# Local attention values: both halves of the sequence in one 64-row product on block-diagonal weights that ScalarE spreads, and weights converted in place

## The chip, the core and the metric

The kernel runs on one NeuronCore of a Trainium2 chip. Its engines are TensorE (PE; its weight loads stand as PEld), VectorE (DVE), ScalarE (ACT), GpSimd (POOL) and SyncE (SP, which issues most of the transfers). The metric is the device time of one execution in microseconds (us); below, it is 401.14 us, the median of three runs (398.07 to 405.84).

## The reference

For 8 batches and 8 heads of 576 positions and 64 numbers each, two attentions are added: a coarse one on means of four positions, and a local one in which a position sees the three before it and the three behind it. The sum goes through a gated causal convolution block.

```python
out_d = sm_attn(q_d, k_d, v_d)            # means over factor = 4 positions, 144 x 144
out_up = np.repeat(out_d, factor, axis=2)
mask = np.abs(pos[:, None] - pos[None, :]) < factor
scores = np.where(mask, scale * q @ k.T, -1e9)
out_local = softmax(scores) @ v
x = (out_up + out_local)                   # -> (8, 576, 512)
gate = sigmoid(causal depthwise convolution of x, 5 taps)
result = (gate * (x @ w_val)) @ w_out
```

w_val, w_out and the taps come in double precision.

## The kernel before

The attention runs in 16 steps. A step i has two pairs of heads (p = 2i and 2i + 1), so four heads. The projections (x @ w_val and h @ w_out) run in blocks of 504 positions, each in pieces of three products per 128 rows: high part by high part, by low part, and low by high (lines 1024 to 1026, tiles `val` and `out`).

**One step.** `sla` and `slb` (lines 682 and 693) make the local scores: the sequence is cut into 24 blocks of 24 queries, each against 30 keys; the tile `sl` holds four combinations of pair and half of the sequence in its four groups of 32 partitions, 12 blocks each for two heads. DVE takes the maximum (`mx`), subtracts it (`sub`, into the tile `ex`), ACT makes the exponentials, DVE sums, inverts, scales (`norm`) and transposes in 32 x 32 squares (`turn`, line 743, tile `pt`). `sd` (line 769) makes the coarse scores, with maximum, exponentials (line 789, into one of two tiles `pd`), scaling (`cnorm`, line 813 on ACT or 815 on DVE) and transpose (`cturn`, line 819, tile `pdt`). `odp` (line 885) makes the coarse values in the tiles `x`, one for each pair, and ACT copies them out (`oc`, line 898, tile `od`). `xa` and `xb` (line 845) then make the local values into the same tiles: for each of 12 blocks, four groups of 32 partitions and two heads, a product with 30 rows, 64 columns of weights from `vw` and 24 moving columns from `pt`; `xa` takes six of the 12 blocks, `xb` the others. DVE adds coarse and local values (`xt`, line 857, 128 x 576 for each pair) when `xb` is done. From there on come a split into high and low part (`xh`, line 916; `xl`, line 920), five convolution taps (lines 929 and 935) and the gate (line 946).

**The weights.** Eight chunks `raw` (in a ring of four buffers, tag `hhl`) come as 64-bit numbers. ACT takes fields of each out (`fld`, lines 971 to 973) into two other tiles, DVE puts them together (`val`, line 976), ACT and DVE or POOL make high and low part (lines 1002 and 1005).

**What sets the order.** `tensor_order()` lists TensorE's work: in `TURN` the scores of step i + 1 stand ahead of the values of step i, with pieces of projection between. A planner then simulates all engines with costs and due times (the numbers in the calls of `op`), lets TensorE take a later entry of the list when one has to wait, picks DVE, POOL or ACT where an operation can go to either, and writes every engine's instructions in a fixed order. It also counts instructions: `CODE` of them make a block of code, for which it assumes a time `FETCH`, and it puts off a phase of many short instructions when it would run out of code by more than `BEAR`. `free` names what must be done before a buffer is used again.

## Time and profile before

| | us |
|---|---|
| median of three runs | 401.14 (398.07 to 405.84) |
| the profiled execution, its time | 400.16 |
| its span, first to last instruction | 398.4 |
| PE busy | 356.5 |
| DVE busy | 309.2 |
| ACT busy | 198.6 |
| POOL busy | 89.7 |

The span is the time between the first and the last instruction of that one execution; the rest of its time lies around it. Busy time is an average over an opening (loads, weight conversion, first steps), a long steady part, and an end in which only projections are left. A PE that is busy can be at half its clock, so the granted clock (1.00 is 2.4 GHz, 0.50 is 1.2 GHz) is read beside it.

### The profile page before, as it was taken

The page shows a single profiled execution, that of the slowest core. Times are in us where ns is not written, and L with a number is a line of the kernel's source. Part 1 is how long each engine was busy: PE and PEld are TensorE (multiplying, and loading weights), DVE is VectorE, ACT ScalarE, POOL GpSimd, SP SyncE. Part 2 cuts the span into 40 slices and gives each one's busy share as a digit, 9 for nine tenths or more (in the row PEclk, how much of TensorE's full clock was granted, in tenths as well). Part 3 has the DMA queues.
Part 4 walks back from the last instruction along what each step waited for, and adds up shares of the span by engine and source line. Part 5 has one row for each costly group of instructions (what it writes and reads, how often), then busy time and mean ns, then how long its engine had stood idle before and what let it go on. Part 6 is the DMA issues. An engine that isn't in the chain of part 4 may idle for free.

```text
span 398.4 us, 15755 instructions
## 1 busy us (share of the span) xinstructions
PE 356.5 (89%) x7055; PEld 279.4 (70%) x7055; DVE 309.2 (78%) x481; ACT 198.6 (50%) x508; POOL 89.7 (23%) x97
## 2 busy tenths in 40 slices
PE   5585659869997989999989999979999999999996
PEld 3464536647775668778667777757777877878996
DVE  7897759993897959998967979995988894935720
ACT  1297259563653544556555544473556462524321
POOL 3223326343123410232103042502240030000000
PEclk9886888987999989999998999998999999999999
DMA  8999997988697979988988979998841301102012
GB/s 226 299 334 233 343 274 154 229 179 203 177 249 174 212 190 218 252 201 209 246 194 181 232 198 268 200 229 197 197 116 55 135 0 52 55 3 77 29 46 74
DMA packets 23476, 71.14 MB, mean 179 GB/s; under 512 B 3185, under 2 KB 9585, under 8 KB 23409
## 3 DMA queue, kind: packets, MB, share of 16 engines
q1 hardware_dynamic: 17504, 52.39, 45.7%
q0 software_dynamic: 5616, 17.50, 24.4%
q8 instruction: 55, 0.90, 1.0%
q10 hardware_dynamic: 288, 0.26, 0.2%
q14 instruction: 13, 0.10, 0.1%
HBM read 60.69 MB, written 9.44 MB: 176 GB/s over the span
## 4 chain that ended last, share of the span: by engine, by line
PE 73%; DVE 11%; issue 7%; DMA 4%; ACT 3%; SPq 1%; ACTq 0%; DVEq 0%
PE out L1024 10%; PE x L845 9%; PE val L1024 8%; PE out L1026 8%; PE out L1025 8%; PE val L1025 7%; PE val L1026 7%; PE sl L693 5%; PE x L885 4%; DMA qk<-in_qk 4%; PE sd L769 4%; DVE gp L935 3%; PE sl L682 1%; DVE h L1052 1%; ACT pd L789 1%
## 5 line engine op out<-in xcount | busy, mean ns | idle before, releaser
L935 DVE SCALAR_TENSOR_TENSOR gp<-xt,cw,gp 128x576 f32<-128x576 f32 x128 | 101.8, 826 | 0.4
L1024 PE MATMUL val<-xhs,wh_v 128*128 128x504 f32 (+1 forms) x160 | 64.5, 403 | 1.5 <-ACT xhs L916 1.5
L1025 PE MATMUL val<-xhs,wl_v 128*128 128x504 f32 (+1 forms) x160 | 60.1, 376 | 2.7 <-issue 2.7
L1024 PE MATMUL out<-hhl,wh_o 128*128 128x504 f32 (+1 forms) x144 | 60.4, 419 | 0.1
L1026 PE MATMUL val<-xls,wh_v 128*128 128x504 f32 (+1 forms) x160 | 60.4, 377 | 0.0
L1026 PE MATMUL out<-hhl,wh_o 128*128 128x504 f32 (+1 forms) x144 | 56.5, 393 | 0.0
L1025 PE MATMUL out<-hhl,wl_o 128*128 128x504 f32 (+1 forms) x144 | 56.3, 391 | 0.0
L845 PEld LDWEIGHTS x<-pt,vw 30*64 30x64 f32 x3072 | 35.3, 133 | 23.9 <-issue 22.1
L857 DVE TENSOR_TENSOR xt<-x,od 128x576 f32<-128x576 f32 x32 | 23.1, 745 | 36.7 <-PE x L845 36.7
L845 PE MATMUL x<-pt,vw 30*64 30x24 f32 x3072 | 39.2, 220 | 12.4 <-issue 12.2
L1115 ACT ACTIVATE ob<-out 128x504 f32<-128x504 f32 (+2 forms) x40 | 21.9, 550 | 42.2 <-PE out L1026 33.9
L693 PE MATMUL sl<-qk 128*24 128x60 f32 x1536 | 30.9, 232 | 12.2 <-DMA qk<-in_qk 7.8
L1066 ACT CAST hhl<-h 128x504 fp32r<-128x504 f32 (+2 forms) x44 | 22.0, 518 | 35.4 <-DVE h L1052 31.4
L693 PEld LDWEIGHTS sl<-qk 128*24 128x24 f32 x1536 | 28.4, 113 | 14.7 <-issue 11.1
L1024 PEld LDWEIGHTS val<-xhs,wh_v 128*128 128x128 f32 x160 | 30.5, 191 | 9.9 <-issue 2.7
L1026 PEld LDWEIGHTS val<-xls,wh_v 128*128 128x128 f32 x160 | 30.5, 191 | 9.1 <-issue 3.2
L576 POOL DMA_DIRECT2D vs<-in_vgr x21 | 18.6, 887 | 79.1 <-DMA vs<-in_vgr 79.1
L1072 POOL TENSOR_TENSOR hhl<-h,hhl 128x504 fp32r<-128x504 f32 (+1 forms) x16 | 20.8, 1306 | 68.8 <-ACT hhl L1066 68.8
L1052 DVE SCALAR_TENSOR_TENSOR h<-gp,val 128x288 f32<-128x288 f32 (+6 forms) x64 | 26.6, 448 | 11.1 <-PE val L1026 10.9
L916 ACT CAST xhs<-xt 128x576 fp32r<-128x576 f32 (+4 forms) x40 | 21.9, 573 | 26.4 <-DVE xt L857 26.2
L1024 PEld LDWEIGHTS out<-hhl,wh_o 128*128 128x128 f32 x144 | 28.3, 196 | 8.0 <-issue 2.3
L1025 PEld LDWEIGHTS val<-xhs,wl_v 128*128 128x128 f32 x160 | 30.7, 192 | 3.8
(82 smaller groups left out, 603.3 us busy)
## 6 DMA issues: line engine op xcount, KB each, us to landing
qk<-in_qk SPq DMA_DIRECT2D x64, 291.0 KB, 8.6
vw<-in_vw SPq DMA_DIRECT2D x16, 768.0 KB, 6.3
qs<-in_qkr POOLq DMA_DIRECT2D x18, 576.0 KB, 9.4
out_t<-ob SPq DMA_DIRECT2D x32, 252.0 KB, 4.8
vs<-in_vgr POOLq DMA_DIRECT2D x21, 320.0 KB, 7.8
qs<-in_qkr SPq DMA_DIRECT2D x6, 576.0 KB, 11.5
vs<-in_vgr SPq DMA_DIRECT2D x7, 320.0 KB, 7.1
raw_v<-in_w_val SPq DMA_DIRECT2D x4, 512.0 KB, 6.9
```

Of the source, the lines that this page charges most:

```text
L693: nc.tensor.matmul(out=sc[32 * q : 32 * q + BQ, 2 * KW * g : 2 * KW * (g + 1)].rearrange("p (h k) -> p h k", h=2), lhsT=t[:, 1, 3 + blk : ...
L845: nc.tensor.matmul(out=s["x", q % 2][64 * hd : 64 * hd + 64, q // 2, BQ * g : BQ * g + BQ], lhsT=s["vw"][32 * q : 32 * q + KW, 2 * g + hd] ...
L857: nc.vector.tensor_tensor(out=xt[:, 4:].rearrange("p (e j r) -> p e j r", e=2, r=FAC), in0=s["x", pr][:, :, 0:HALF].rearrange("p e (j r) - ...
L916: nc.scalar.copy(out=xhs[:, c, g : g + t - f], in_=s["xt"][:, 4 + f : 4 + t])
L935: nc.vector.scalar_tensor_tensor(out=s["gp"], in0=s["xt"][:, k : k + S], scalar=cw[:, c, k : k + 1], in1=s["gp"], op0=ALU.mult, op1=ALU.add,)
L1024: nc.tensor.matmul(out=o, lhsT=wh[:, d, col], rhs=his[d], start=d == 0, stop=False)
L1025: nc.tensor.matmul(out=o, lhsT=wl[:, d, col], rhs=his[d], start=False, stop=False)
L1026: nc.tensor.matmul(out=o, lhsT=wh[:, d, col], rhs=los[d], start=False, stop=d == NC - 1)
L1052: nc.vector.scalar_tensor_tensor(out=t["h"][:, cs], in0=st[b * NC + c]["gp"][:, f:e], scalar=1.0, in1=box["o"][:, cs], op0=ALU.add, op1=AL ...
L1066: nc.scalar.copy(out=t["hh"][:, cuts[n]], in_=t["h"][:, cuts[n]])
L1072: eng.tensor_tensor(out=t["hl"][:, cs], in0=t["h"][:, cs], in1=t["hh"][:, cs].bitcast(F32), op=ALU.subtract)
L1115: nc.scalar.mul(t["ob"][:, cs], box["o"][:, cs], 0.5)
```

## The change

The local values are made by products of 64 rows instead of 30. The pair of heads now decides which 64 partitions a score lies in, and the half of the sequence which 32 of these. After the transpose ACT copies `pt` into a new tile `pt2`, which has two groups of 24 columns: the first half's rows go to the first group and the second half's rows to the second, and the rest, zeroed once, stays zero. So one product with 64 rows and 48 moving columns gives both halves of the sequence. `xa` and `xb` have half as many products, of twice the columns. The four copies (`spr0` to `spr3`, 32 partitions each) wait for `turn` and for `xa` and `xb` of the step before; `xa` waits for them.

The result of `xa` and of `xb` lies in a bank of its own, and the addition becomes four operations of 128 x 288 (`xu` after `xa`, `xt` after `xb`) in place of two of 128 x 576. The two tiles `pd` become one, so that the exponentials of the coarse scores wait for `cturn` of the step before. The weight fields are written into the 64-bit chunk itself, which is held until the low part is made. Five costs of the planner and its rule for a switch between kinds of work differ; they have an effect through the order alone.

```diff
-CODE, FETCH, BEAR = 256, 4500, 300
+CODE, FETCH, BEAR = 256, 5500, 300
-        return 0 if a == b else 95
+        return 0 if a == b else (95 if b != "P" else 30)
-    pds = [cpool.tile([P, NG, 32 * NB], F32, name=f"pd{i}") for i in range(2)]
+    pt2 = cpool.tile([P, 2 * NI, 2, BQ], F32, name="pt2")
+    pd = cpool.tile([P, NG, 32 * NB], F32, name="pd")
+        nc.gpsimd.memset(pt2, 0.0)
...
-                        t = st[pair[q % 2]]["qk"]
-                        blk = HALF * (q // 2) + BQ * (NI // 2 * part + g)
+                        t = st[pair[q // 2]]["qk"]
+                        blk = HALF * (q % 2) + BQ * (NI // 2 * part + g)
...
+        def spread(q):
+            def run():
+                r = slice(32 * q, 32 * q + 32)
+                nc.scalar.copy(out=pt2[r, :, q % 2], in_=s["pt"][r, :, 0:BQ])
...
-        op(("turn", i), "DVE", 870, turn, [("norm", i)], free=[("xa", i - 1), ("xb", i - 1)])
+        op(("turn", i), "DVE", 870, turn, [("norm", i)], free=spreads(i - 1))
+        for k, q in zip(spreads(i), range(4)):
+            op(k, "ACT", 560, spread(q), [("turn", i)], free=[("xa", i - 1), ("xb", i - 1)])
...
-            op(k, "ACT", 283, exp(g), [("cbi", i)] + exps[:g][:1], free=[("cturn", i - 2)])
+            op(k, "ACT", 283, exp(g), [("cbi", i)] + exps[:g][:1], free=[("cturn", i - 1)])
...
-                for g in range(NI // 2 * part, NI // 2 * (part + 1)):
-                    for q in range(4):
-                        for hd in range(2):
+                for g in range(NI // 2):
+                    n = 2 * (NI // 2 * part + g)
+                    for pr in range(2):
+                        for hd, r in enumerate((LO, HI)):
                             nc.tensor.matmul(
-                                out=s["x", q % 2][64 * hd : 64 * hd + 64, q // 2, BQ * g : BQ * g + BQ],
-                                lhsT=s["vw"][32 * q : 32 * q + KW, 2 * g + hd],
-                                rhs=s["pt"][32 * q : 32 * q + KW, 2 * g + hd, 0:BQ],
+                                out=s["x", pr][r, part, 0:HALF].rearrange("p (e g j) -> p e g j", e=2, j=BQ)[:, :, g],
+                                lhsT=s["vw"][(LO, HI)[pr], n + hd],
+                                rhs=pt2[(LO, HI)[pr], n + hd],
...
-        op(("raw", q), "SP", 620, dma, free=[("fld", q - RAWB)], size=P * 512 * 8)
-        op(("fld", q), "ACT", 1700, fields, [("raw", q)], free=[("wlo", q - 2), ("val", q - 1)])
+        op(("raw", q), "SP", 620, dma, free=[("wlo", q - RAWB)], size=P * 512 * 8)
+        op(("fld", q), "ACT", 1700, fields, [("raw", q)])
```

TensorE in step 5, from the last coarse products through two pieces of projection into `xa`, before (a row that ends in x2 stands for the two heads; `out1_0` is a tile of block 1's result):

```order
L885 MATMUL x1_5_2082<-pdt5_1982,vs2_841 64x145 x2
L1024 MATMUL out1_0_1976<-hhl1_3_1984,wh_o_95 128x504
L1025 MATMUL out1_0_1976<-hhl1_3_1984,wl_o_96 128x504
L1026 MATMUL out1_0_1976<-hhl1_3_1984,wh_o_95 128x504
L1024 MATMUL out1_1_1987<-hhl1_3_1984,wh_o_95 128x504
L1025 MATMUL out1_1_1987<-hhl1_3_1984,wl_o_96 128x504
L1026 MATMUL out1_1_1987<-hhl1_3_1984,wh_o_95 128x504
L845 MATMUL x0_5_2081<-pt5_1937,vw5_1605 64x24 x2
L845 MATMUL x1_5_2082<-pt5_1937,vw5_1605 64x24 x2
```

The same place of the changed kernel:

```order
L902 MATMUL x1_5_1857<-pdt5_1778,vs2_702 64x145 x2
L1040 MATMUL out1_0_1782<-hhl1_3_1780,wh_o_93 128x504
L1041 MATMUL out1_0_1782<-hhl1_3_1780,wl_o_94 128x504
L1042 MATMUL out1_0_1782<-hhl1_3_1780,wh_o_93 128x504
L1040 MATMUL out1_1_1792<-hhl1_3_1780,wh_o_93 128x504
L1041 MATMUL out1_1_1792<-hhl1_3_1780,wl_o_94 128x504
L1042 MATMUL out1_1_1792<-hhl1_3_1780,wh_o_93 128x504
L858 MATMUL x0_5_1856<-pt2_76,vw5_1408 64x2x24 x2
L858 MATMUL x1_5_1857<-pt2_76,vw5_1408 64x2x24 x2
```

The two pieces stay where they were. The rows of line 845 go on to 24 for `xa`, those of line 858 to 12, and each of the latter has two groups of 24 columns.

ACT between the exponentials of step 11's and of step 12's local scores, before (`ex` is the tile of the local weights, `od` the copy of the coarse values, `hhl` and `xhs` high parts, `gp` the gate):

```order
L725 ACTIVATE ex_75<-ex_75 128x24x30
L783 ACTIVATE cbi11_3742<-cmx11_3730 128x5
L789 ACTIVATE pd1_77,csm11_3744<-sd11_3701,cbi11_3742 128x144 x5
L1066 CAST hhl4_0_3774<-h4_0_3736 128x504
L898 COPY od0_10_3780<-x0_10_3748 128x144
L898 COPY od1_10_3782<-x1_10_3749 128x144
L946 ACTIVATE gp18_3673<-gp18_3673 128x576
L1066 CAST hhl4_1_3848<-h4_1_3841 128x504
L946 ACTIVATE gp19_3690<-gp19_3690 128x576
L1066 CAST hhl4_2_3928<-h4_2_3875 128x504
L916 CAST xhs_86<-xt0_82 128x144
```

The changed kernel from the same `hhl` of block 4 on:

```order
L1082 CAST hhl4_2_3447<-h4_2_3418 128x504
L933 CAST xhs_86<-xt0_82 128x144
L933 CAST xhs_86<-xt0_82 128x432
L946 ACTIVATE gp20_3467<-xt0_82,cw_90 128x576
L754 COPY pt2_76<-pt11_3460 32x24x24 x3
L825 ACTIVATE pd_77<-pd_77,crs11_3542 128x144 x5
L1082 CAST hhl4_3_3563<-h4_3_3534 128x252 x2
L754 COPY pt2_76<-pt11_3460 32x24x24
L933 CAST xhs_86<-xt1_83 128x144
```

The four copies of line 754 stand among the casts, with five scalings of `pd` and two casts between the third and the fourth. Over the whole program the planner also deals some work out anew: of the 40 subtractions `xl`, DVE has 32 instead of 22 and POOL 8 instead of 18; of the subtractions `hlo`, DVE has 9 fewer and POOL 9 more; three of the 16 `norm` go from DVE to POOL; and of the 16 `cnorm`, ACT has 14 instead of 11 (five instructions each).

## Rows read from the trace of the kernel before

**Rows 1.** The page's busy times: engine, us, share of the span, instructions.

```profile
PE 356.5 (89%) x7055; PEld 279.4 (70%) x7055; DVE 309.2 (78%) x481; ACT 198.6 (50%) x508; POOL 89.7 (23%) x97
```

**Rows 2.** Busy us of each engine by stretch of the span, granted clock, transfers' share, GB/s.

```profile
36.00:90.00 54.00, 39.16 (x938) 28.36 (x937) 46.23 (x67) 32.19 (x76) 22.86 (x21) 0.85 0.94 236
90.00:343.00 253.00, 242.87 (x5034) 188.15 (x5033) 208.95 (x330) 130.49 (x348) 57.64 (x57) 0.97 0.75 181
```

**Rows 3.** Waits of PE from 90 to 343 us: line, released by, us, times, longest.

```profile
PE x L845 <- issue: 5.3, 3, 2.4
PE val L1025 <- issue: 2.7, 2, 2.3
PE sd L769 <- issue: 1.2, 3, 0.7
PE sl L693 <- issue: 0.4, 1, 0.4
```

**Rows 4.** The longest waits of PE on issue from 0 to 90 us.

```profile
PE x L845 <- issue: 6.9, 2, 3.5
PE sl L693 <- issue: 3.9, 1, 3.9
PE out L549 <- issue: 3.8, 1, 3.8
```

**Rows 5.** The longest wait of DVE from 90 to 343 us.

```profile
DVE xt L857 <- PE x L845: 25.6, 9, 5.2
```

**Rows 6.** PE in order of time: start us, us, line, operation, count [idle before].

```profile
119.60 1.15 PE L845 MATMUL x<-pt,vw 30*64 30x24 f32 x96
120.69 0.50 PE L1024 MATMUL val<-xhs,wh_v 128*128 128x504 f32 x1
...
129.65 0.80 PE L693 MATMUL sl<-qk 128*24 128x60 f32 x48
130.38 0.50 PE L1024 MATMUL out<-hhl,wh_o 128*128 128x504 f32 x1
...
157.71 1.43 PE L769 MATMUL sd<-qs 64*32 64x144 f32 x40
159.06 0.50 PE L1024 MATMUL val<-xhs,wh_v 128*128 128x504 f32 x1
...
209.48 0.47 PE L845 MATMUL x<-pt,vw 30*64 30x24 f32 x18 [1.54 <-issue]
```

**Rows 7.** The page's queue of code transfers: packets, MB, share of 16 engines.

```profile
q8 instruction: 55, 0.90, 1.0%
```

**Rows 8.** Two of three stretches at half clock behind such waits, columns as above.

```profile
144.80:148.20 3.40, 3.40 (x10) 2.69 (x9) 0.83 (x2) 0.68 (x1) 0.63 (x2) 0.50 0.51 190
...
267.70:271.10 3.40, 3.40 (x9) 2.64 (x8) 0.65 (x1) 0.45 (x1) 0.86 (x1) 0.50 0.64 184
```

**Rows 9.** Groups of instructions by line: count, busy us, mean ns, idle before.

```profile
L845 PE MATMUL x<-pt,vw 30*64 30x24 f32 x3072 | 39.2, 220 | 12.4 <-issue 12.2
L857 DVE TENSOR_TENSOR xt<-x,od 128x576 f32<-128x576 f32 x32 | 23.1, 745 | 36.7 <-PE x L845 36.7
L813 ACT ACTIVATE pd<-pd,crs 128x144 f32<-128x144 f32 x55 | 18.0, 404 | 9.9 <-DVE crs L807 9.7
L971 ACT ACTIVATE bits_v<-raw_v 128x512 uint16<-128x512 uint32 x4 | 3.2, 790 | 0.0
L973 ACT ACTIVATE a_v<-raw_v 128x512 f32<-128x512 f32 x4 | 2.6, 660 | 0.0
```

**Rows 10.** Groups by line with shapes kept apart: DVE from PSUM at 288 columns, ACT.

```profile
L1052 DVE SCALAR_TENSOR_TENSOR h<-gp,val 128x288 f32<-128x288 f32 x16 | 7.2, 450 | 1.4 <-PE val L1026 1.4
L916 ACT CAST xhs<-xt 128x576 fp32r<-128x576 f32 x24 | 15.9, 668 | 17.8 <-DVE xt L857 17.7
```

**Rows 11.** DVE and then PE in step 7, in order of time.

```profile
171.92 0.97 DVE L743 STREAM_TRANSPOSE pt<-ex 128x768 f32<-128x768 f32 x1
...
182.33 1.15 PE L845 MATMUL x<-pt,vw 30*64 30x24 f32 x96
```

More of the change, by code (lines that the diff above doesn't have):

```diff
@@ L669, in tile_two_scale_attn_gated_conv, with spreads @@
     at = {}
+    def spreads(i):
+        return [(f"spr{q}", i) for q in range(4)]
     def local_scores(i):
@@ L789, in run @@
                 nc.scalar.activation(
-                    out=pds[i % 2][:, g, 0:SD],
+                    out=pd[:, g, 0:SD],
                     in_=s["cs"][:, g],
@@ L863, in combine @@
             return run
-        op(("xa", i), "PE", 850, mm(0), [("vw", i), ("turn", i), ("odp", i), ("oc0", i), ("oc1", i)], cols=(576, 290), code=192)
-        op(("xb", i), "PE", 850, mm(1), [("xa", i)], cols=(576, 290), code=192)
+        op(("xa", i), "PE", 700, mm(0), [("vw", i), ("odp", i), ("oc0", i), ("oc1", i)] + spreads(i), cols=(1150, 290), code=96)
+        op(("xb", i), "PE", 700, mm(1), [("xa", i)], cols=(1150, 290), code=96)
         for pr in range(2):
             p = 2 * i + pr
-            op(
-                (f"xt{pr}", i), "DVE", 680, combine(pr), [("xb", i), (f"oc{pr}", i)],
-                free=[("tap3", p - 4), ("xl", p - 4)],
-            )
+            for part, (k, x) in enumerate((("xu", "xa"), ("xt", "xb"))):
+                op(
+                    (f"{k}{pr}", i), "DVE", 390, combine(pr, part), [(x, i), (f"oc{pr}", i)] + [(f"xu{pr}", i)] * part,
+                    free=[("tap3", p - 4), ("xl", p - 4)],
+                )
     def coarse_av(i):
@@ L903, in coarse_av @@
         op(
-            ("odp", i), "PE", 1200, mm, [("vb", i) if i < 2 else ("vs3", i // 2), ("cturn", i)],
-            banks=[("a", [(f"xt{pr}", i)]) for pr in range(2)], cols=(1450, 144), code=80,
+            ("odp", i), "PE", 1250, mm, [("vb", i) if i < 2 else ("vs3", i // 2), ("cturn", i)],
+            banks=[("a", [(f"xu{pr}", i), (f"xt{pr}", i)]) for pr in range(2)], cols=(1450, 144), code=80,
         )
@@ L963, in tile_two_scale_attn_gated_conv, with f64_parts @@
     whl = {}
-    def f64_parts(src, bits, at):
+    def f64_parts(src):
         w = src.bitcast(U32).rearrange("p (n two) -> p n two", two=2)
-        lo, hi = w[:, :, 0], w[:, :, 1].bitcast(F32)
-        low, top = (bits.bitcast(t).rearrange("p (n two) -> p n two", two=2)[:, :, i] for i, t in enumerate((U16, I16)))
+        lo, at = w[:, :, 0], w[:, :, 1]
+        hi = at.bitcast(F32)
+        low, top = (src.bitcast(t).rearrange("p (n four) -> p n four", four=4)[:, :, i] for i, t in enumerate((U16, I16)))
         def fields():
@@ L992, in fields @@
         def fields():
-            t["a"] = work.tile([P, 512], U32, tag="h", name=f"a_{nm}{d}")
-            bits = work.tile([P, 512], U32, tag="ob", name=f"bits_{nm}{d}")
-            t["f"] = f64_parts(t["raw"], bits, t["a"])
+            t["f"] = f64_parts(t["raw"])
             t["f"][0]()
@@ L1082, in val_unit @@
         two = units.index((j, c)) - 2
-        held = [("wlo", 2 * NC - 2), ("wlo", 2 * NC - 1)] if j == 0 else []
         op((f"h{c}", j), "DVE", 75 + w * 574 // 504 + 60 * (len(batches) - 1), gated,
            [(f"v{c}.{pieces(j) - 1}", j)] + [("gate", b * NC + c) for b in batches],
-           free=held + [(f"hlo{units[two][1]}.{n}", units[two][0]) for n in range(2) if two >= 0])
+           free=[(f"hlo{units[two][1]}.{n}", units[two][0]) for n in range(2) if two >= 0])
         hfree = [(f"o{NC - 1}.{NC - 1}", j - 1) if j <= NFULL else (f"v{NC - 1}.{NC - 1}", NFULL - 1)]
         if j == 0:
-            hfree = [("fld", 2 * NC - 1 - i) for i in range(RAWB)]
+            hfree = [("wlo", 2 * NC - 1 - i) for i in range(RAWB)]
         if c == NC - 1 and j < NFULL:
@@ L1143, in cw_in @@
         nc.sync.dma_start(out=cw_raw, in_=conv_w)
-    cw_low, cw_at = (cpool.tile([P, NC * 5], U32, name=n) for n in ("cw_low", "cw_at"))
-    cw_parts = f64_parts(cw_raw, cw_low, cw_at)
+    cw_parts = f64_parts(cw_raw)
     def cw_value():
         cw_parts[1]()
-        nc.vector.tensor_copy(out=cw2, in_=cw_at.bitcast(F32))
+        nc.vector.tensor_copy(out=cw2, in_=cw_parts[2])
     op(("cwf", 0), "SP", 620, cw_in, size=P * NC * 5 * 8)
@@ L1210 @@
     v2 = v.reshape(NSTEP, 2, 2, S, D)
-    vp = np.pad(v2, ((0, 0), (0, 0), (0, 0), (3, 5), (0, 0)))
-    vw = np.stack([vp[:, :, :, BQ * g : BQ * g + 32] for g in range(2 * NI)], axis=3)
-    vw = vw.reshape(NSTEP, 2, 2, 2, NI, 32, D).transpose(0, 3, 1, 5, 4, 2, 6).reshape(NSTEP, P, 2 * NI, D)
+    vp = np.pad(v2, ((0, 0), (0, 0), (0, 0), (3, 3), (0, 0)))
+    vw = np.stack([vp[:, :, :, BQ * g : BQ * g + KW] for g in range(2 * NI)], axis=3)
+    vw = np.pad(vw, ((0, 0), (0, 0), (0, 0), (0, 0), (0, 32 - KW), (0, 0)))
+    vw = vw.reshape(NSTEP, 2, 2, 2, NI, 32, D).transpose(0, 1, 3, 5, 4, 2, 6).reshape(NSTEP, P, 2 * NI, D)
     vg = np.pad(v.reshape(B, 2, 2, 2, SD, FAC, D), ((0, 0), (0, 0), (0, 0), (0, 0), (0, 32 * NB - SD), (0, 0), (0, 0)))
```

47 lines of the change are left out of this document (25 added, 22 removed).

## The prediction

> **What bounds the kernel now.** I read the busy times by stretch first. From 90 to 343 us PE is busy for 242.9 of 253 us, DVE for 209.0 (83%), ACT for 130.5 (52%) [rows 2]. So in the long steady part TensorE sets the pace, and DVE comes next. From 36 to 90 us it is the other way round: DVE 46.2 of 54 us, PE 39.2, and PE's clock is 0.85 of full speed on the mean [rows 2].
>
> Then the waits. From 90 to 343 us PE waits for no other engine; all four rows name "issue", where the profile sees nothing that was waited for, 9.6 us in sum [rows 3]. DVE's longest wait there is for PE, in `xt`, 25.6 us [rows 5]. Before 90 us the three long waits on issue are 6.9, 3.9 and 3.8 us [rows 4].
>
> What is it that PE waits for on "issue"? One queue of transfers carries instructions, 55 packets of 0.90 MB, so 16.4 KB each [rows 7]. PE and PEld have 14,110 instructions [rows 1], 256.5 for each packet. So I read these packets as TensorE's code, 256 instructions at a time. A wait on issue cuts an x phase in two: 18 of its 96 products come 1.54 us late [rows 6]. Such a phase of 192 instructions takes 1.09 us, and a piece of projection has six instructions in a good half microsecond. Dense phases use code up fastest, and `xa` and `xb` are the densest. The Trainium skill's page "Runtime: NRT & Kernel Launch", Instruction fetch mechanics, agrees on blocks of 256 instructions, but says that the fetch is hidden behind the sequencer's own pace. By that the waits have another cause, and the change leaves them; the second rival below is that case.
>
> Three stretches of 3.4 us from 90 us on have a granted clock of 0.50, so 1.2 GHz instead of 2.4, and they come up to 4 us after a wait in an x phase [rows 8].
>
> **The change, part by part.**
>
> *x phases.* Before, 96 products go in 1.09 us, from 119.60 to the next projection at 120.69 [rows 6]. What limits them? Two phases with four places of the array in use show what columns cost: 40 products of 144 columns take 1.35 us, 48 of 60 columns 0.73 us [rows 6]. That is ten rounds of four at 144 and twelve at 60; the difference, 0.62 us for 720 columns, gives 0.86 ns a column and leaves 0.11 us for the ends of a phase. An x phase of before has eight places and twelve rounds of 24 columns, 0.25 us by columns, so columns don't limit it. It goes at (1.09 - 0.11) / 96 = 10.2 ns a product, which I take as the pace of issue. Afterwards there are 48 products of 48 columns in four places: twelve rounds, 12 x 48 x 0.86 = 0.50 us by columns and 48 x 10.2 = 0.49 us by issue, with the ends 0.60 us. That is the lower bound. The upper bound takes the 82 ns of a round of before as the latency of one place, to which 24 more columns add 21 ns: 12 x 103 ns and the ends, 1.34 us. I take 0.70: near the lower end, since the phase of 144 columns runs in the same pattern of four places without such a latency, and a little over it, since two limits that lie together seldom overlap fully. So 0.39 us less for each of 32 phases. 26 of them (13 steps) lie behind 90 us: **10.1 us**. The other six give 2.3, of which I count a quarter, as in the opening below: **0.6**.
>
> The Trainium skill's page "TensorEngine Tiling (Array Packing)", Theoretical Speedup, speaks against this: its gain goes with the number of tiles, and the change has four where there were eight, half filled with zeros. If a phase went by places, it would take twice its 0.98 us; the trace has a quarter of that as column time, so here it doesn't.
>
> *Waits on issue.* PE's instructions fall by 3,072 to 11,038, or 43 packets; an x phase has 96 instead of 192. Of the 9.6 us behind 90 us, 5.3 are in x phases and 2.7 in a projection [rows 3], which I take to be behind one. I take three quarters of these 8.0 as gone and a third of the other 1.6: **6.6 us** (bounds 0 and 9.6).
>
> *Clock.* Each stretch of 3.4 us at half clock costs 1.7 us. If two of three waits before them go, so do they: **3.4 us** (bounds 0 and 5.1).
>
> *The opening.* 14.6 us of waits on issue lie before 90 us [rows 4], but DVE is busy for 86% of the stretch from 36 on, so I count a quarter: **3.7 us** (bounds 0 and 12).
>
> *Four copies on ACT.* The nearest row is a cast of 128 x 576 in 668 ns [rows 10], also 576 elements in a partition: 64 x 0.67 = 43 us. With 15 more scalings of `pd` at 404 ns [rows 9], 6 us, ACT goes from 198.6 to 248 us, 65% of a span of 380. The copies lengthen the way from `pt` to `xa` by 2.7 us. Their cover is the distance that lies there now: in step 7 the transpose ends at 172.89 and `xa` begins at 182.33, 9.4 us later [rows 11], and the order of PE between the coarse values and `xa` is the same in the step shown. So I take nothing. Without the cover it would be 2.7 us a step. Queued behind a copy that waits for `turn` are casts, scalings and, further on, the copies of results out of PSUM.
>
> *Four additions for two.* A DVE operation on 128 x 288 from PSUM takes 450 ns [rows 10], the addition of 128 x 576 takes 745 [rows 9]: 1.80 instead of 1.49 us a step, 5.0 us in all on DVE. In return `xu` can start an x phase earlier. The planner's new dealing takes ten `xl` to DVE and nine `hlo`, three `norm` and three `cnorm` away from it; I take this as even, within 3 us either way. PE waits for neither now, so it costs nothing by itself.
>
> *DVE's share.* Here the gain meets its limit. The four terms shorten the stretch of 253 us by 10.1 + 6.6 + 3.4 = 20.1 to 233 us, in which DVE has 209 us and some 4 more of additions, 91%. The engines take their work in a fixed order, so at such a share some of its delays reach PE. The slack that is left is DVE's wait for PE, 25.6 us [rows 5], and the gain would use four fifths of it. I give back a quarter of 20.1: **-5.0 us** (bounds 0 and 10).
>
> *One tile `pd`.* The exponentials of step i + 1 now wait for `cturn` of step i; since `odp` of step i needs that transpose anyway and stands right behind `sd` of step i + 1, I take nothing, at the upper end the 1.35 us of an `sd` phase in a few steps.
>
> *Weights in place.* Fields are written at a step of two or four words. Field reads of that kind take 660 ns, and 790 with 16-bit results [rows 9]; the 0.13 us between them for eight chunks and four operations is 4 us at most, spread over ACT and DVE in the opening. Chunks are held for three operations longer, about 2 us, before w_out may come. ACT, 32.2 of 54 us busy [rows 2], hides the one, and in the opening the order asks for w_out only after all of block 0's values. I take nothing.
>
> The sum: 10.1 + 0.6 + 6.6 + 3.4 + 3.7 - 5.0 = 19.4 us. The profiled execution takes 400.16 us, so 380.8; the median of the three runs, 401.14, lies 1 us higher, so I say **381 us**, 5% less.
>
> **The rivals.**
>
> *It does what it says, and more (6%).* DVE gives nothing back and the opening gains fully: 19.4 + 5.0 + 8 = 32 us, **368 us**. For it speaks that PE's order is hardly changed; against it, that DVE is busy for 86% of the opening.
>
> *The waits on issue stay (14%).* Then only the x phases count, 10.7 us, and DVE needs nothing back: **389 us**, up to 394 if an x phase takes 0.85. For it speaks the page's rule above, and that 14.6 of the waits lie in an opening that has many transfers; against it the agreement of 14,110 and 55 packets.
>
> *The x phase doesn't get shorter (8%).* Its time was a latency of places: 1.34 us, 0.25 more for 32 phases, 8 us. Less code still gives 6.6 + 3.4 + 3.7: **395 us**. Against it is the phase with 144 columns.
>
> *Slower: ACT's copies come late (12%).* The place is ACT's queue between `turn` and `xa`. If DVE, at 91%, makes `turn` late, the copies hold ACT, and what stands behind them (copies of results, high parts) holds PE. All of 2.7 us exposed in 13 steps is 35 us: 380.8 + 35 = **416 us**. It decides from (19.4 + 8) / 13 = 2.1 us a step, when the kernel is over 2% slower. For it speaks that ACT's load grows by a quarter; against it the 9.4 us of cover.
>
> **How the numbers follow.** The forecast, between 368 and 388, has 60%; the rivals have 6, 14, 8 and 12%. About 2% is what a measurement of this kernel can tell from no change, so "faster" ends at 393. Forecast, first rival and two thirds of the second, 9 of its 14%, make 75% faster; the rest of the second and the third make 13% the same; the last 12% is slower. The range leaves out the last rival, the first one's far side and what lies above 394: **368 to 394 us**.
>
> **What would show it.** An x phase takes 0.6 to 0.8 us from its start to the next projection; 1.0 or more refutes the first term. The waits of PE on issue behind 90 us come to 3 us or less, and the instruction packets to about 43; if the packets fall and the waits don't, code isn't their cause. At most one stretch after 90 us has half clock, the end apart. DVE's share of the steady part goes to about 90%, and its wait for PE in `xt` shrinks; if waits of PE for DVE or ACT come up there by more than 8 us, my give-back is too small. Between the last copy and `xa` some microseconds are left. The prediction is wrong if the opening grows, since I have no term for that.

## The result, and the profile after

The changed kernel takes 378.25 us (median of four runs, 375.37 to 379.75); the kernel before takes 403.49 us beside it (398.07 to 410.04). The ratio is 0.946, with a 95% interval from 0.934 to 0.958, so it is 5.4% faster. Medians are over all runs, but ratios leave out slow runs, those over 1.5% above the fastest of the same kernel, so 378.25 / 403.49 is not quite the ratio. The profiled execution takes 377.33 us with a span of 375.6, against 400.16 and 398.4 before.

The page of the changed kernel: the busy times, and the queue that carries instructions (packets, MB, share of the time of 16 transfer engines).

```profile
PE 344.2 (92%) x5518; PEld 269.2 (72%) x5518; DVE 308.8 (82%) x508; ACT 254.9 (68%) x587; POOL 91.2 (24%) x99
...
q8 instruction: 43, 0.70, 0.8%
```

PE and PEld together have 3,074 instructions fewer than in [rows 1], and the queue carries 43 packets instead of 55 [rows 7]. ACT goes from 198.6 to 254.9 us.

Busy us by stretch, with granted clock, transfers' share and GB/s, of the changed kernel; the third stretch is the only one behind 90 us with a granted clock near a half before the tail's end.

```profile
36.00:90.00 54.00, 41.61 (x758) 30.09 (x757) 50.51 (x72) 46.99 (x85) 19.86 (x17) 0.87 0.95 243
90.00:320.00 230.00, 226.72 (x3870) 176.10 (x3870) 204.70 (x351) 168.85 (x418) 61.76 (x63) 0.99 0.82 198
...
124.70:128.10 3.40, 3.40 (x58) 2.38 (x60) 1.11 (x3) 1.46 (x4) 1.78 (x2) 0.51 0.95 262
```

The stretch from 90 to 320 us answers to the one from 90 to 343 before [rows 2]: PE is now busy for 99% of it instead of 96, DVE for 89% instead of 83. In the opening, DVE has gone from 46.2 to 50.5 of 54 us and ACT from 32.2 to 47.0.

The waits of PE in the changed kernel from 90 to 320 us (line, released by, us, times, longest), all above 0.15 us:

```profile
PE x L858 <- issue: 1.8, 1, 1.8
PE out L1040 <- ACT ob L1130: 0.8, 1, 0.8
PE sl L697 <- issue: 0.2, 1, 0.2
PE out L1040 <- DVE crs L819: 0.2, 1, 0.2
PE x L858 <- ACT od L915: 0.2, 1, 0.2
```

The 9.6 us of [rows 3] have become 2.0. The other waits are 1.2 us in sum.

Where did the time go? I followed the last product of each step's `xb` in the records. In both kernels it begins at nearly the same time for step 2, at 85.1 us before and at 84.8 after. For step 15 it is 363.0 and 340.1. The x phases in which these products lie, of step 2 (`xa` and `xb` together) and of step 15 (`xb`), before and then after:

```profile
83.17 2.17 PE L845 MATMUL x<-pt,vw 30*64 30x24 f32 x192
362.01 1.15 PE L845 MATMUL x<-pt,vw 30*64 30x24 f32 x96
...
83.05 1.93 PE L858 MATMUL x<-pt,vw 64*64 64x48 f32 x96
339.41 0.92 PE L858 MATMUL x<-pt,vw 64*64 64x48 f32 x48
```

So the opening gave nothing (of the projections, 51 products were done by then before and 48 after), and the 13 steps behind it went from 277.9 to 255.3 us: 22.6 us of the span's 22.8 lie there. The tail is equal, 35.4 and 35.5 us. These 13 steps split up so:

- The waits on issue in them were 13.4 us (the 9.6 of [rows 3] and one of 3.8 at 85.7 us, which [rows 4] counts to the opening) and are 2.0: 11.4 us.
- An x phase takes 0.84 us instead of 1.09: 26 x 0.25 = 6.5 us.
- Stretches at half clock in them were 17.0 us (three of 3.4, of which [rows 8] has two, and the one of 6.8 below) and are 3.4. PE worked for 14.3 us of the 17.0, since in the one of 6.8 it was still waiting on issue at first, which is counted above: (14.3 - 3.4) / 2 = 5.5 us.
- New waits of PE for other engines: -1.2 us.

The sum is 22.2 of 22.6 us.

The stretch of 6.8 us at half clock in the kernel before:

```profile
86.80:93.60 6.80, 4.09 (x12) 3.04 (x13) 4.40 (x6) 3.20 (x6) 2.70 (x3) 0.50 1.02 250
```

TensorE in step 5 of the changed kernel (start us, us, engine, line, operation), `xa` and the next piece of projection:

```profile
137.84 0.92 PE L858 MATMUL x<-pt,vw 64*64 64x48 f32 x48
138.68 0.49 PE L1040 MATMUL out<-hhl,wh_o 128*128 128x504 f32 x1
```

From 137.84 to 138.68 are the 0.84 us; `xb` of the step takes the same, from 142.29 to 143.13.

### The profile page after: what moved, and what is told of

Its sections match the earlier page's. It is cut to its first block, busy times and chain, and to the rows that moved or that the text cites. A ratio compares the mean times of both kernels' runs of the same rounds, so it can differ in the third digit from the quotient of the medians.

```text
span 375.6 us, 12811 instructions
## 1 busy us (share of the span) xinstructions
PE 344.2 (92%) x5518; PEld 269.2 (72%) x5518; DVE 308.8 (82%) x508; ACT 254.9 (68%) x587; POOL 91.2 (24%) x99
## 4 chain that ended last, share of the span: by engine, by line
PE 68%; DVE 12%; ACT 11%; DMA 4%; issue 2%; POOL 1%; SPq 1%; ACTq 0%; POOLq 0%; DVEq 0%
PE out L1040 10%; PE val L1040 9%; PE out L1042 8%; PE out L1041 8%; PE val L1042 7%; PE val L1041 7%; PE x L858 6%; PE x L902 4%; PE sd L781 4%; PE sl L697 4%; DVE gp L952 4%; DMA vs<-in_vgr 3%; DMA raw<-in_vgr 2%; ACT raw_v L990 1%; ACT pt L754 1%
## 5 line engine op out<-in xcount | busy, mean ns | idle before, releaser
L952 DVE SCALAR_TENSOR_TENSOR gp<-xt,cw,gp 128x576 f32<-128x576 f32 x128 | 103.4, 839 | 4.7 <-ACT gp L946 4.3
L1040 PE MATMUL out<-hhl,wh_o 128*128 128x504 f32 (+1 forms) x144 | 58.1, 404 | 1.0 <-ACT ob L1130 0.8
L1042 PE MATMUL out<-hhl,wh_o 128*128 128x504 f32 (+1 forms) x144 | 54.7, 380 | 0.0
L1041 PE MATMUL out<-hhl,wl_o 128*128 128x504 f32 (+1 forms) x144 | 54.6, 379 | 0.0
L754 ACT COPY pt<-pt 32x576 f32<-32x576 f32 x64 | 42.9, 670 | 10.4 <-PE x L858 6.4
L1088 POOL TENSOR_TENSOR hhl<-h,hhl 128x504 fp32r<-128x504 f32 (+1 forms) x25 | 29.3, 1205 | 53.7 <-ACT hhl L1082 47.1
L697 PE MATMUL sl<-qk 128*24 128x60 f32 x1536 | 30.0, 229 | 9.4 <-DMA qk<-in_qk 8.9
L858 PEld LDWEIGHTS x<-pt,vw 64*64 64x64 f32 x1536 | 27.2, 141 | 12.8 <-issue 6.3
L963 ACT ACTIVATE gp<-gp 128x576 f32<-128x576 f32 x32 | 22.0, 688 | 20.5 <-DVE gp L952 20.1
L873 DVE TENSOR_TENSOR xt<-x,od 128x288 f32<-128x288 f32 x64 | 26.0, 443 | 11.7 <-PE x L858 11.2
L1040 PEld LDWEIGHTS out<-hhl,wh_o 128*128 128x128 f32 x144 | 27.0, 188 | 9.1 <-issue 2.5
```

The lines of the kernel that those rows point to most:

```text
L697: nc.tensor.matmul(out=sc[32 * q : 32 * q + BQ, 2 * KW * g : 2 * KW * (g + 1)].rearrange("p (h k) -> p h k", h=2), lhsT=t[:, 1, 3 + blk : ...
L754: nc.scalar.copy(out=pt2[r, :, q % 2], in_=s["pt"][r, :, 0:BQ])
L858: nc.tensor.matmul(out=s["x", pr][r, part, 0:HALF].rearrange("p (e g j) -> p e g j", e=2, j=BQ)[:, :, g], lhsT=s["vw"][(LO, HI)[pr], n + h ...
L873: nc.vector.tensor_tensor(out=xt, in0=s["x", pr][:, part, 0:HALF].rearrange("p (e j r) -> p e j r", e=2, r=FAC), in1=od.broadcast_to([P, 2 ...
L952: nc.vector.scalar_tensor_tensor(out=s["gp"], in0=s["xt"][:, k : k + S], scalar=cw[:, c, k : k + 1], in1=s["gp"], op0=ALU.mult, op1=ALU.add,)
L963: nc.scalar.activation(out=s["gp"], in_=s["gp"], func=AF.Tanh, scale=0.5)
```

## Experiments

Two questions decide why it is faster: is it the time of the x products or the code they need, and which limit holds an x phase at 0.84 us? Two more are on ACT's copies and on the opening, where nothing was gained. Times of this and the kernel before are medians of one comparison; the kernel before varies from 403 to 410 us between them, so ratios are read across comparisons, and times within one. The changed kernel itself has a ratio of 0.946 above and of 0.926 (0.920 to 0.933) as the control below, so a ratio carries over from one comparison to another only to some 2%.

**The planner's numbers.** The change also has new costs for the planner, `FETCH` and a cheaper switch among them. Two kernels set them apart from the products. The first is the changed kernel with the old numbers.

```diff
-CODE, FETCH, BEAR = 256, 5500, 300
+CODE, FETCH, BEAR = 256, 4500, 300
-        return 0 if a == b else (95 if b != "P" else 30)
+        return 0 if a == b else 95
-        op(("xa", i), "PE", 700, ...
+        op(("xa", i), "PE", 850, ...     (and the old costs of xb, sla, slb, sd, odp)
```

> The changed kernel with the planner numbers of before: 950, 950, 1200, 1200 for scores and coarse values, 850 for xa and xb, 95 for every switch, FETCH 4500. Theory (products and code): within 2% of the changed kernel, 372 to 386 us, waits of PE on issue behind 90 us up to 5 us. Rival (the order brings the gain): 391 us or more.

Measured: 378.91 us (377.26 to 380.20) beside 409.48, ratio 0.928 (0.920 to 0.936). Its queue carries 43 packets too, and the list of its waits behind 90 us has only 0.3 us on issue (and 4.3 us for DVE). The second is the kernel before with the new numbers, those of `sla`, `slb`, `sd`, `odp` and the switch, and a `FETCH` of 5200, since with the 5500 of the changed kernel the planner finds no order for the old products (the cut shows two of the edits).

```diff
-CODE, FETCH, BEAR = 256, 4500, 300
+CODE, FETCH, BEAR = 256, 5200, 300
-        return 0 if a == b else 95
+        return 0 if a == b else (95 if b != "P" else 30)
```

> The kernel before with the changed kernel's planner numbers: 720, 720, 1240 and 1250 for the scores and coarse values, 30 for the switch to a projection, and FETCH 5200 instead of 4500 (from 5400 on the planner finds no order for the old products). Theory (the gain comes from the products: a shorter x phase and less code): within 2% of before, 55 code transfers, waits of PE on issue behind 90 us above 5 us. Rival (the order that the numbers give brings it): 4% or more below before, waits on issue of 3 us or less.

Measured: 422.72 us (421.45 to 425.05) beside 408.32, ratio 1.042 (1.034 to 1.050). In some of its steps the planner puts warming products between `xa` and `xb`, which write over columns of `xa`'s result; no work is left out. Its packets, and the first of its waits of PE from 90 to 364 us:

```profile
q8 instruction: 56, 0.92, 0.9%
...
PE x L845 <- issue: 21.3, 8, 4.1
```

What follows: with the new products the numbers make no difference that was measured, and with the old products these numbers, in an order of their own, cost 4%. The gain is that of the products. The second kernel also shows how much the old x phases can lose on issue: eight waits, of up to 4.1 us.

**Code or time.** If the instructions of an x phase are what costs, then giving them back without much time must bring back the waits; if its time is, then time without instructions must cost as much. One kernel issues 48 tiny products of 32 weight columns and 8 moving ones ahead of each x phase (so 96 instructions, as many as were saved), the other five wide ones (10 instructions). Both write into columns that nothing reads.

```diff
+                for k in range(48):
+                    nc.tensor.matmul(
+                        out=s["x", 0][32 * (k % 4) : 32 * (k % 4) + 32, part, 480:488],
+                        lhsT=ident_b[:, 32 * (k % 4) : 32 * (k % 4) + 32],
+                        rhs=mask_b[:, 0:8], start=True, stop=True)
```

> The changed kernel, its order kept, with 48 tiny products (32 columns of weights, 8 moving columns, to PSUM columns that nothing reads) ahead of the products of each x phase: as much code as before (some 55 code transfers) and 0.5 to 0.6 us more in each phase, 13 to 16 us behind 90 us. Theory (code that comes late is what PE waits for on issue): waits on issue behind 90 us come back, 8 us or more, with stretches at half clock behind them, and the time is 400 us or more. Rival (those waits have another cause): waits on issue stay under 4 us and the time is the time of the products alone, 389 to 394 us.

```diff
+                for k in range(5):
+                    nc.tensor.matmul(
+                        out=s["x", 0][:, part, HALF:512], lhsT=ident_b,
+                        rhs=mask_b[:, 0 : 512 - HALF], start=True, stop=True)
```

> The changed kernel, its order kept, with five wide products (128 x 128 weights, 224 moving columns, to PSUM columns that nothing reads) ahead of the products of each x phase: about 0.5 us more in each phase, as with the tiny ones, but only ten instructions. Both theories: waits on issue behind 90 us under 4 us; 26 phases of 0.5 us behind 90 us make 13 us, so 389 to 394 us if PE sets the pace there; 378 to 385 us if PE has slack that the profile hides.

Measured in one comparison with 409.48 us before: the tiny products 415.96 us (413.76 to 417.05), ratio 1.019 (1.012 to 1.027); the wide ones 392.41 us (390.28 to 394.25), ratio 0.962 (0.953 to 0.971). The kernel with the tiny products: packets, the stretch from 90 to 360 us, PE's waits in it above 1.0 us, and an x phase that is cut in two.

```profile
q8 instruction: 55, 0.90, 0.9%
...
90.00:360.00 270.00, 252.94 (x5224) 197.97 (x5212) 213.01 (x362) 174.47 (x426) 65.65 (x65) 0.96 0.72 174
...
PE x L866 <- issue: 7.3, 4, 3.8
PE x L855 <- issue: 3.1, 2, 2.5
PE sl L697 <- issue: 2.2, 2, 1.5
PE val L1048 <- issue: 1.5, 1, 1.5
PE val L1048 <- ACT ob L1138: 1.2, 1, 1.2
...
146.43 0.51 PE L855 MATMUL x<-mask_b,ident_b 128*32 128x8 bf16 x48
146.87 0.55 PE L866 MATMUL x<-pt,vw 64*64 64x48 f32 x18
148.76 0.68 PE L866 MATMUL x<-pt,vw 64*64 64x48 f32 x30 [1.35 <-issue]
```

The kernel with the wide products, the same views:

```profile
q8 instruction: 44, 0.72, 0.8%
...
90.00:333.00 243.00, 240.09 (x4007) 187.32 (x4006) 208.04 (x354) 172.03 (x422) 63.60 (x64) 1.00 0.78 191
...
PE sd L781 <- issue: 2.4, 1, 2.4
PE out L1048 <- ACT ob L1138: 0.3, 1, 0.3
...
140.56 0.66 PE L855 MATMUL x<-mask_b,ident_b 128*128 128x224 bf16 x5
141.14 0.92 PE L866 MATMUL x<-pt,vw 64*64 64x48 f32 x48
```

From its start to the `xa` behind it, a group of tiny products takes 0.44 us and a group of wide ones 0.58. So the kernel with the tiny products adds less of TensorE's own time and is 23.5 us slower. What it has more is code: 55 packets, as many as before, waits on issue as before, and after them a mean clock of 0.96 against 1.00. This is the clearest result: at equal order and slightly more time of their own, 86 instructions fewer a phase are worth 6%. The wide products show the other half. Their 0.58 us, 26 times, are 15.1 us; steps 3 to 15 take 265.8 us instead of 255.3, 10.5 more, although a stretch at half clock is gone (1.7 us), and the whole is 13.5 us above the changed kernel with old numbers in the same comparison. So most of TensorE's time shows: TensorE sets the pace of these steps.

The records of the code packets show the wait itself. In the 14 traces of this case PE waits on issue 39 times for 0.7 us or more, and each of these waits ends 1.2 to 1.6 us after a packet of the instruction queue has landed, where the packets come 6.8 to 9.0 us apart on the mean of a trace. They also stand where a block of code begins: in the kernel before, between one of its eight such waits and the next lie 254, 510, 1274, 1270, 762, 2796 and 2286 recorded instructions of TensorE, each within 4 of a whole multiple of 254.

The Trainium skill's page "Runtime: NRT & Kernel Launch", Instruction fetch mechanics, says that this fetch is hidden behind the sequencer's pace. For these dense phases the two kernels speak against it, by their 23.5 us, and so do the 39 waits.

**What holds an x phase at 0.84 us.** The prediction took the columns and the issue as limits, 0.60 us. Two kernels change one size each: one moves 24 columns instead of 48, the other loads 32 weight columns into a place instead of 64. Both leave half of the local values out, and both fill the rest with four wide products in the coarse phase.

```diff
-                                rhs=pt2[(LO, HI)[pr], n + hd],
+                                rhs=pt2[(LO, HI)[pr], n + hd, 0],
```

> The changed kernel in which each product of the local values takes 24 moving columns instead of 48, so the second half of the sequence is left out (four fill products in the coarse values' phase give its columns a value and lengthen that phase by half a us). In the changed kernel a round of four products takes 58 ns and a phase 0.84 us. Theory (a round is bound by the loads of 64 weight columns, which begin only when the products before them have begun): the round stays at 55 to 60 ns, the phase at 0.80 to 0.86 us. Rival (moving columns bound it): 0.60 to 0.68 us.

```diff
-                                out=s["x", pr][r, part, 0:HALF]...
-                                lhsT=s["vw"][(LO, HI)[pr], n + hd],
+                                out=s["x", pr][64 * hd : 64 * hd + 32, part, 0:HALF]...
+                                lhsT=s["vw"][(LO, HI)[pr], n + hd, 0:32],
```

> The changed kernel in which each product of the local values takes 32 weight columns instead of 64, so half of each head's 64 numbers are left out (with the same fill products in the coarse values' phase). Theory (a round is bound by its weight loads): the round falls to 43 to 48 ns and the phase to 0.62 to 0.70 us. Rival (moving columns, or a fixed latency of a place): the phase stays at 0.80 to 0.86 us.

Measured, one run each: 382.59 and 377.97 us. Timeline of TensorE with 24 moving columns:

```profile
231.37 0.90 PE L858 MATMUL x<-pt,vw 64*64 64x24 f32 x48
232.19 0.50 PE L1045 MATMUL val<-xhs,wh_v 128*128 128x504 f32 x1
```

And with 32 weight columns:

```profile
232.18 0.71 PE L858 MATMUL x<-pt,vw 64*32 64x48 f32 x48
232.82 0.49 PE L1045 MATMUL val<-xhs,wh_v 128*128 128x504 f32 x1
```

Half the moving columns leave the phase at 0.82 us; half the weight columns bring it to 0.64, though as many instructions are issued and as many columns move. So neither columns nor issue hold the changed kernel's x phase: the load of 64 weight columns does. (With the weight columns the partitions of the result are halved as well; that these bound the round is not excluded by a run, but half the columns of the result, in the kernel with 24 moving columns, changed nothing.) With the 0.11 us for the ends that the prediction worked out, a round of four products takes (0.84 - 0.11) / 12 = 61 ns, and 44 ns with 32 weight columns, which is close to the 41 ns that 48 moving columns take at 0.86 ns; that these are the limit then was not tested. The Trainium skill's page "TensorE: Matmul & The Clock Gate", LDWEIGHTS, says that a load's time goes by its columns and not by its rows, columns / 1.2 in ns; as an estimate that is 53 ns for 64. The trace agrees within 8 ns, if the loads of four places overlap.

**ACT's copies.** The prediction put them at no cost, since 9.4 us lay between transpose and `xa`. Two kernels change that one load. One makes each copy twice:

```diff
-                nc.scalar.copy(out=pt2[r, :, q % 2], in_=s["pt"][r, :, 0:BQ])
+                for _ in range(2):
+                    nc.scalar.copy(out=pt2[r, :, q % 2], in_=s["pt"][r, :, 0:BQ])
```

> The changed kernel with each of the 64 copies on ACT made twice, 43 us more on ACT, 2.7 us more a step between the transpose and the local values. Theory (the copies are hidden in the steady part; only the opening feels ACT): no new wait of PE for ACT in xa behind 90 us, 1 to 3 us a step lost in the three steps of the opening at most, 379 to 387 us. Rival (ACT's queue is near the bound): 13 steps of 1 to 2.7 us, 391 to 413 us.

The other, from step 1 on, copies one of 24 blocks, so that two thirds of their time are gone, 0.21 us each instead of 0.67 and 26 us less on ACT (the local values are then those of old weights).

```diff
+                n = 2 * NI if i == 0 else 1
-                nc.scalar.copy(out=pt2[r, :, q % 2], in_=s["pt"][r, :, 0:BQ])
+                nc.scalar.copy(out=pt2[r, 0:n, q % 2], in_=s["pt"][r, 0:n, 0:BQ])
```

> The changed kernel, its order kept, in which the four copies of each step after the first take one of 24 blocks instead of all (the other blocks keep the first step's values): some 28 us less on ACT. Making each copy twice cost 33 us; this asks what making it once costs. Theory (a single copy is covered, the queue behind it has room for one and not for two): 1 to 6 us less than the changed kernel, most of it in the opening, 370 to 377 us. Rival (the cost goes with the copies): 15 us less or more, 363 us or less.

Measured: twice gives 410.38 us (409.24 to 414.10), ratio 1.012 (1.004 to 1.020), where the changed kernel itself, run again in the same comparison as a control, has 377.65 (373.71 to 379.38), ratio 0.926 (0.920 to 0.933).

> The changed kernel once more, as the yardstick for the other kernels of this comparison: 375 to 381 us, ratio to before between 0.925 and 0.955.

One of 24 blocks gives 378.83 us (377.14 to 382.27), ratio 0.936 (0.928 to 0.943). In the profiled executions steps 3 to 15 take 254.8 us with it, and 255.3 and 252.1 in the two of the changed kernel. So one copy costs nothing that was measured, and a second costs 33 us. The kernel with two copies, from 90 to 354 us: the longest waits of PE, and some of the longest of DVE.

```profile
PE x L859 <- ACT od L916: 8.9, 6, 2.6
PE val L1041 <- ACT ob L1131: 4.0, 2, 2.4
...
DVE gp L953 <- ACT gp L947: 16.5, 7, 5.6
DVE sm L733 <- ACT ex L729: 11.7, 5, 3.5
DVE xls L938 <- ACT xhs L934: 7.8, 7, 2.6
```

Here my theory of the cover fell. Four second copies are 2.7 us a step, well within 9.4. But the waits aren't for `pt2`, whose last copy still ends 3.0 us or more ahead of `xa` in every step: PE waits for `od` and `ob` and DVE for the gate, the exponentials and the high parts, all of them work that stands behind the copies in ACT's queue. Steps 3 to 15 take 280.8 us instead of the control's 252.1, so 28.7 / 13 = 2.2 us a step of the 2.7. Of the 28.7, waits of PE make some 18 and half clock some 9: these steps have 17.8 us of it and the control none, so a good part of the price is the clock behind the waits. What counts is the room that is left in ACT's queue, not the distance from the copy to its reader: at 254.9 us busy the copies fit, at 295.9 they hold up what stands behind them. Where between the two the room ends was not measured. The prediction's last rival had the mechanism (what stands behind the copies is late) and nearly the price (2.7 us a step), only not its point: it comes with the second copy.

**The opening.** There, waits on issue went as they should, and others came. The longest waits of PE in the changed kernel from 0 to 90 us, and the fields of a weight chunk on ACT (busy us, mean ns of one):

```profile
PE sl L697 <- DMA qk<-in_qk: 8.9, 4, 3.4
PE x L902 <- DVE pdt L831: 5.7, 1, 5.7
PE val L1040 <- ACT xhs L933: 3.3, 2, 2.1
PE x L550 <- ACT od L915: 2.7, 1, 2.7
...
PE sl L697 <- issue: 0.2, 1, 0.2
...
L989 ACT ACTIVATE raw_v<-raw_v 128x512 uint16<-128x512 uint32 x4 | 5.4, 1343 | 0.0
L990 ACT ACTIVATE raw_v<-raw_v 128x512 int16<-128x512 f32 x4 | 5.4, 1356 | 0.1
L991 ACT ACTIVATE raw_v<-raw_v 128x512 f32<-128x512 f32 x4 | 2.6, 656 | 0.1
```

The two fields with 16-bit results take 1.35 us each instead of 0.79 [rows 9], and are now written at a step of four half-words instead of two: 16 x 0.56 = 9 us more on ACT. They are also written over their own source; that it is the step and not this was not tested apart, but the third field, written in place too, takes 656 ns instead of 660. Is that what keeps the opening from gaining? The first kernel undoes this part alone (the cut shows two of its edits; the tiles, the buffers and what they wait for go back too, and the planner's order changes with them).

```diff
-        low, top = (src.bitcast(t).rearrange("p (n four) -> p n four", four=4)[:, :, i] ...
+        low, top = (bits.bitcast(t).rearrange("p (n two) -> p n two", two=2)[:, :, i] ...
-            nc.scalar.activation(out=hi, in_=hi, func=AF.Copy, scale=2.0**-112)
+            nc.scalar.activation(out=at.bitcast(F32), in_=hi, func=AF.Copy, scale=2.0**-112)
```

> The changed kernel with the weights converted as before, into two other tiles instead of in place. In the changed kernel's trace the two field operations with 16-bit results take 1.36 us instead of 0.79 and ACT is busy for 47.0 of the 54 us from 36 to 90. Theory (in-place fields cost ACT 9 us in the opening and took the gain there): those operations take 0.79 us again, the opening up to the last product of step 2's local values is 3 us or more shorter, and the time is 1% or more below the changed kernel, 375 us or less. Rival (DVE or the loads bound the opening): the opening ends within 2 us of the changed kernel's and the time stays within 1%.

Measured, beside the control's 377.65: 373.83 us (373.34 to 376.31), ratio 0.922 (0.917 to 0.926). One of its fields, and its opening:

```profile
L988 ACT ACTIVATE bits_v<-raw_v 128x512 uint16<-128x512 uint32 x4 | 3.1, 781 | 0.0
...
36.00:90.00 54.00, 41.63 (x756) 30.51 (x757) 48.46 (x72) 36.03 (x82) 18.00 (x18) 0.81 0.98 248
```

The field is back at 0.78 us and ACT at 36.0 of 54. The end of step 2's `xb`, by which the opening was to be judged, comes later and not earlier, at 88.0 us against 84.4, but the new order has 57 projection products done by then instead of 48. By step 3's `xb`, with as many of them done in each (87), it is at 100.1 us where the control is at 102.6: 2.5 us, of the fields and the new order together. The whole is 1% less than the control, but the two intervals overlap, so a loss of 1% by this part is not shown beyond the spread.

The second kernel adds to this a cheaper spread: two copies over all 128 partitions, each scaled by a column of ones and zeros, in place of four over 32 (the cut leaves out how the column is made).

```diff
-                nc.scalar.copy(out=pt2[r, :, q % 2], in_=s["pt"][r, :, 0:BQ])
+                nc.scalar.mul(pt2[:, :, q], s["pt"][:, :, 0:BQ], half[:, q : q + 1])
```

> The changed kernel with the weights converted into two other tiles as before, and with two copies a step instead of four: each takes all 128 partitions and multiplies by a column of ones and zeros, so that a copy writes its half's rows and zeros the others. 32 copies of 0.67 us instead of 64, 21 us less on ACT, besides the 9 us of the fields. Theory (ACT is what the opening waits for, and the copies hold up its queue): 364 to 371 us, ACT at 225 us or less, the last product of step 2's local values at 82 us or earlier. Rival (the opening is bound by DVE or the loads, and the copies were covered): 372 to 376 us, as with the weights alone.

Measured: 373.58 us (371.72 to 380.19) beside 406.30, ratio 0.921 (0.915 to 0.927). ACT falls to 223.8 us, and the time is that of the kernel with the old fields alone, as the rival said; step 2's `xb` ends at 87.2 us and not at 82. Its median is 1% below the changed kernel's, within the spread; less load on ACT brings no more, which agrees with the kernel that copies one of 24 blocks.

The third takes DVE's load in the opening down instead: the means over four positions read one position; the other three are left out (one of two such edits is shown).

```diff
-                    t = s["qk"][:, 1, 3 : 3 + S].rearrange("p (j r) -> p j r", r=FAC)
+                    t = s["qk"][:, 1, 3 : 3 + S].rearrange("p (j r) -> p j r", r=FAC)[:, :, 0:1]
```

> The changed kernel, its order kept, in which the 16 pooling sums of the opening on DVE (0.74 and 1.34 us each) read one of four positions instead of all, so the coarse scores of the first two batches are not the means: some 10 us less on DVE before 80 us. Theory (DVE, busy for 50 of the 54 us from 36 to 90, is what the opening waits for, so less code on TensorE gave nothing there): the last product of step 2's local values comes at 79 us or earlier instead of 84.4, and the time is 367 to 373 us. Rival (loads or ACT set the opening): 82 us or later, 374 us or more.

Measured: 379.44 us (374.95 to 380.95), ratio 0.938 (0.925 to 0.952). Its reductions and its longest wait of PE behind the loads, 0 to 90 us:

```profile
L661 DVE TENSOR_REDUCE qs<-qk 128x144 f32<-128x288 f32 x8 | 5.4, 680 | 0.0
L658 DVE TENSOR_REDUCE qs<-qk 128x144 f32<-128x144 f32 x8 | 3.3, 410 | 1.4 <-DMA qk<-in_qk 1.3
...
PE x L902 <- DVE pdt L831: 7.3, 1, 7.3
```

They take 680 and 410 ns instead of 1335 and 740, 7.9 us less on DVE, and step 2's `xb` ends at 85.1 us, as without it. So DVE's load alone doesn't set the opening, and ACT's copies alone don't either (87.1 us with one of 24 blocks). The chain of work through the opening of the changed kernel goes from one engine to the other (start us, us):

```profile
54.73 1.25 ACT raw_o L989
...
70.13 1.76 DVE gp L952
...
76.98 0.92 DVE pdt L831
```

Fields of w_out on ACT stand ahead of the gate's taps on DVE, and these ahead of `pdt`, for which PE waits. Only the two kernels with shorter fields, which also have another order, were earlier by step 3. Which of the loads, ACT and DVE bounds the opening stays open; the three were not changed together.

## Why the prediction was right, and where it was not

The forecast was 381, in a range of 368 to 394; it came to 378.25, and the profiled execution fell by 22.8 us where the sum had 19.4. That the change works by less code and shorter x phases, and that TensorE sets the pace, is shown by the two kernels of code and time. But single terms missed by up to 5 us and made up for each other, so that the total came this close is in part luck.

- *x phases, 10.1 us behind 90 us.* 6.5 measured. The phase takes 0.84 us, within the bounds of 0.60 and 1.34, and not 0.70. The failed step is "near the lower end": it left out a limit, the load of 64 weight columns into a place. The phase of 144 columns that it leaned on could not show it: its products load 32 weight columns (the 64*32 of [rows 6]), and 144 x 0.86 = 124 ns of moving columns hide even a load of 60. The place-count rule that it weighed and set aside would have had the phase grow; it fell from 1.09 to 0.84.
- *Waits on issue, 6.6 us.* (Three quarters of 8.0 and a third of 1.6 are 6.5.) 7.6 behind 90 us, and 3.8 at 85.7 us; in the control, a second execution of the changed kernel, none are left there. The reading of 55 packets as 256 instructions each gave 43 afterwards, and 43 there are. That a packet is what PE waits for is shown by the tiny products, with 55 packets and waits of up to 3.8 us, and by the landing of packets 1.2 to 1.6 us ahead of the end of every long wait.
- *Clock, 3.4 us.* One stretch is left of the three behind 90 us, as said; that is 3.4. The fourth, at 86.8 to 93.6 us before, went too and was counted to the opening; with 4.1 us of work in it, it cost 2.0.
- *The opening, 3.7 and 0.6 us.* Nothing, to step 2's `xb`. Its waits on issue went and others for DVE and ACT took their place: the prediction let three quarters of the gain go to this, and the whole went. The step that failed is "I take nothing" for the weights in place: ACT had 9 us more of fields, because the step of the results was costed by the step of the reads. ACT went to 47.0 of 54 us, so its cover was gone. Undone, it gives 2.5 us back by step 3, with the reservations above: another order goes with it, and in the whole time it is not shown. What bounds the opening stays open.
- *The give-back by DVE, -5.0 us.* It did not come. DVE's share rose to 89% (90 to 91 said), its wait for PE in `xt` fell from 25.6 to 4.9 us as said, and yet PE waits for DVE for 0.2 us. A quarter was a guess without a row; at 89% this order still has its slack.
- *Four additions for two.* 443 ns each, 450 said.
- *Copies on ACT, nothing.* Right in size, 670 ns each, 42.9 us, and in cost: taking two thirds of them away gains nothing that was measured. As said, some microseconds are left between the last copy and `xa`, from 3.2 to 16.1. But the reason given was not the whole one: the room in ACT's queue covers them, not only the 9.4 us, and one more set of copies uses it up.
- *The rivals.* "The waits on issue stay" is out by the 2.0 us that are left, "the x phase doesn't get shorter" by 0.84. The slower one didn't come here, but the kernel with two sets of copies is its case: 410.38 us, where the rival had worked out 416 and 2.1 us a step as the point from which the kernel is 2% slower; 2.2 were measured, at 1.2% slower.

## What to carry to other kernels

Where PE waits on "issue" in dense phases of small products, count instructions against the packets of the instruction queue, and test it with tiny products that add code without time: here the 86 instructions a phase by which two such kernels differ were worth 23.5 us, where the shorter phases gave 6.5. Before costing packed small products by columns, cost the load of the weights of one place too. Whether added work on a helper engine is hidden is asked of that engine's whole queue, and answered by doubling the work: the first dose cost nothing that was measured, the second 33 us.

## What the runs showed of the hardware

- A round of four fp32 products of 64 rows in four places takes, as estimated from the phases (0.84, 0.82 and 0.64 us for twelve rounds, less 0.11 for the ends), 61 ns with 64 weight and 48 moving columns, 59 with 24 moving columns, and 44 with 32 weight columns.
- Waits on instructions come inside an x phase though it has only 96 instructions (1.35 us after 18 of 48 products), and behind 90 us they reach 3.8 us with 55 packets, 4.1 us with 56. All 39 of 0.7 us or more end 1.2 to 1.6 us after a packet of 16.4 KB has landed.
- ACT's 16-bit results take 1.35 us for 128 x 512 written at a step of 8 bytes and 0.78 at a step of 4; the 32-bit result at 8 bytes takes 0.66.
